# Attention and a mixture of eight experts on one core: when the expert weights are fetched

## The chip, the cores and the metric

The kernel runs on one core of one Trainium2 chip. The metric is the device time of one execution in microseconds (us), less is better. The profile is one execution recorded by the hardware profiler; times in it count from the start of its span.

## The reference

Attention over 4 batches, 8 heads, 768 positions and 64 dimensions a head: three heads attend to everything before them, five only to the first 4 positions and a window of 64. Its output is laid out as 3072 tokens of 512 values, and each token goes through the one expert that its `domain_id` names.

```
scores = where(mask, q @ k.T / sqrt(64), -1e9)       # per batch and head, 768 x 768
attn   = softmax(scores) @ v
x = attn.transpose(0, 2, 1, 3).reshape(3072, 512)    # token, model dimension
for e in range(8):                                   # w1[e]: 512 x 1024, w2[e]: 1024 x 512
    mask = domain_id == e
    out[mask] = relu(x[mask] @ w1[e]) @ w2[e]
```

## The kernel before

**Attention.** The work is cut into 16 steps `n`: 4 batches by 4 pairs of heads. SyncE (SP) loads q, k and v in fp32, GpSimd (POOL) casts them to fp16, TensorE (PE) transposes q and k and multiplies, ScalarE (ACT) takes the exponential, VectorE (DVE) divides and writes the batch's rows into `xb`. After the last step of a batch `store_x` (line 410) sends `xb` to the DRAM tensor `x_tok` through SP's DMA queue. `hooks(n)` (line 751) is called ahead of step `n` and issues the loads and casts of later steps. Its table `ws` (line 764) names the steps at which a weight transfer is issued. At step 14 it issues the first four token gathers, which need only the first three batches.

**Experts.** While attention runs, VectorE works out which token goes to which slot: each expert has 448 slots, two experts make a pair, a pair is seven groups of 128 slots. `load_xe(pr, g)` (line 627) gathers the rows of one group from `x_tok` by an indirect DMA; `x_transpose` (line 640) turns a group so that `layer1(e, c0, c1)` (line 662) can multiply it by `w1` and ScalarE apply the relu; `layer2(e)` (line 697) and `layer2_half(pr)` (line 711) multiply by `w2`, and `finish_group` (line 682) copies 128 result rows to an `oute` tile on VectorE and scatters them to the output by an indirect DMA. The `oute` tiles have 4 buffers, the PSUM tiles of layer 2 have 2.

**Weights.** `load_w(e, 1)` and `load_w(e, 2)` (line 178) fetch `w1[e]` and `w2[e]`. Each reads 2048 KB of fp32 and lands 1024 KB of fp16, so each is a DMA that casts, and GpSimd issues it. There are four buffers for `w1` and four for `w2`; the fifth transfer of a kind waits until the first expert's matmuls have been done.

**What sets the order.** The schedule is written by hand: every engine executes its instructions in the order in which the code emits them. So gathers, weight transfers and scatters all stand in one line on GpSimd, and their packets in one DMA queue (q0 in the profile). The DMAs of this queue use eight completion semaphores in turn (DMASW0 to DMASW7 below): each DMA's issue waits until the DMA eight places ahead of it has landed, and everything behind it on GpSimd waits too.

**The code around the change.** After attention, lines 798 to 830: `store_x(3)`; the gathers of the last three groups (2, 6, 5) of pair 0; `layer1` of experts 0 and 1 on the first 256 slots; the seven gathers of pair 1; five weight transfers; the transposes of groups 2, 6, 5; `layer1` of experts 0 and 1 on their last 192 slots, each followed by a transfer of `w1` for expert 4 or 5; and then the loop over the experts. In iteration `e` of that loop `layer1(e + 2)` stands ahead of `layer2(e)`, even iterations begin with the seven transposes of the next pair and the seven gathers of the pair after it. Two lines show the loop's transfers of weights:

```
            if nxt + 4 < E: load_w(nxt + 4, 1)     # line 826, behind layer1(nxt)
        if e + 4 < E: load_w(e + 4, 2)             # line 829, behind layer2(e)
```

## Time and profile before

| | us |
|---|---|
| median of 3 runs (lowest, highest) | 257.03 (255.66, 266.19) |
| the profiled execution | 254.73 |
| its span | 253.0 |
| busy in the span: PE, VectorE, GpSimd, ScalarE | 202.8, 105.5, 110.2, 92.6 |

The profile's page gives busy time by engine, the span in 40 slices with the clock that the throttle granted to TensorE, the DMA queues and the costliest groups of instructions. Behind the page stand views of the trace: who waited for whom; the instructions of an engine in order of time; the instructions of one line with the time from issue to landing of its DMAs; and busy time, granted clock and DMA share in chosen stretches. In the order of time, brackets at a row's end give the engine's idle time before that row and what ended it. Attention ends near 104 us of the span, the experts' part fills the rest.

### The profile page before, as it was taken

Reading aid. Unit: us, or ns where it says so; the run is one execution under the profiler, and the core shown is the slowest. Engines: PE = TensorE matmul, PEld = TensorE weight load, DVE = VectorE, ACT = ScalarE, POOL = GpSimd, SP = SyncE. Lnnn points to the kernel's source line nnn. Section 1 sums busy time; section 2 is a strip of 40 time slices with the busy share of each in tenths; the row PEclk is TensorE's granted clock in tenths of the full one; section 3 lists DMA queues with packets and bytes.
Section 4 is the critical chain, followed back from the end, with each engine's and each line's share of the span. In section 5 each row is a group of like instructions: output and inputs, shape, how many; then the busy total and the mean of one; then the engine's idle time right before and its main releaser. Section 6 shows DMA issues by size and latency. Waiting matters only on the chain. (4 is left out here: it accounts for less than half of the span.)

```text
span 253.0 us, 4605 instructions
## 1 busy us (share of the span) xinstructions
PE 202.8 (80%) x1871; PEld 120.8 (48%) x1871; DVE 105.5 (42%) x242; ACT 92.6 (37%) x109; POOL 110.2 (44%) x143
## 2 busy tenths in 40 slices
PE   1589899988999999869604999507899979999960
PEld 0246556655666666869401545203545445454420
DVE  1259999997578576501400031004222150403330
ACT  2277547744875876253200504100222305050000
POOL 0557564562455523067932122364757140414550
PEclk9999959997999999997955899956999999999995
DMA  6999999999999842233599999899995856212421
GB/s 218 299 311 305 285 294 254 329 322 244 293 325 226 153 142 72 78 109 97 109 214 216 211 216 216 209 227 237 271 265 174 167 155 135 92 36 84 156 86 37
DMA packets 45467, 49.77 MB, mean 197 GB/s; under 512 B 27263, under 2 KB 38784, under 8 KB 45442
## 3 DMA queue, kind: packets, MB, share of 16 engines
q0 software_dynamic: 7936, 26.75, 45.9%
q1 hardware_dynamic: 36928, 22.02, 31.6%
q10 hardware_dynamic: 578, 0.66, 0.9%
q8 instruction: 16, 0.26, 0.4%
q14 instruction: 9, 0.07, 0.1%
HBM read 56.76 MB, written 10.49 MB: 266 GB/s over the span
## 5 line engine op out<-in xcount | busy, mean ns | idle before, releaser
L332 ACT ACTIVATE eT<-sp 128x1024 f16<-128x1024 f32 (+2 forms) x68 | 60.5, 916 | 35.4 <-PE sp L311 34.8
L678 ACT ACTIVATE hT<-h 128x896 f16<-128x896 f32 (+2 forms) x40 | 30.7, 768 | 96.1 <-PE h L671 96.1
L671 PE MATMUL h<-xT,w 128*128 128x448 f16 (+2 forms) x320 | 54.0, 331 | 11.6 <-DMA w<-in_moe_w_dram 10.8
L684 DVE COPY oute<-o 128x512 f32<-128x512 f32 x24 | 16.6, 692 | 88.5 <-PE o L702 70.1
L702 PE MATMUL o<-w,hT 128*128 128x512 f16 x192 | 44.4, 389 | 10.0 <-DVE oute L684 10.0
L631 POOL DMA_INDIRECT xe<-x_tok,map_i x28 | 28.4, 1013 | 47.9 <-DMA w<-in_moe_w_dram 23.8
L671 PEld LDWEIGHTS <-w 128*128 128x128 f16 x320 | 35.2, 117 | 29.3 <-DMA w<-in_moe_w_dram 11.0
L686 POOL DMA_INDIRECT out_dram<-oute,out_i x28 | 27.9, 997 | 42.4 <-DVE oute L684 37.1
L702 PEld LDWEIGHTS <-hT 128*128 128x128 f16 x192 | 19.0, 99 | 33.6 <-issue 12.4
L386 PE MATMUL av<-ve,eT 128*128 128x65 f16 (+3 forms) x532 | 31.8, 198 | 3.2 <-DVE xb L399 3.2
L386 PEld LDWEIGHTS <-eT 128*128 128x128 f16 (+3 forms) x572 | 25.9, 101 | 13.8 <-issue 4.1
L311 PE MATMUL sp<-qT,kT 64*128 64x192 f16 (+6 forms) x244 | 26.7, 282 | 1.8 <-DVE kT L281 1.2
L311 PE MATMUL sp<-c16s 128*128 128x128 f16 (+1 forms) x132 | 25.9, 279 | 0.4 <-ACT eT L332 0.3
L155 POOL CAST q<-q 128x768 f16<-128x768 f32 x15 | 12.9, 862 | 30.6 <-PE tpq L276 14.5
L281 DVE COPY qT<-tpq 128x768 f16<-128x768 f16 x16 | 15.3, 954 | 7.6 <-PE tpq L276 7.5
L399 DVE TENSOR_TENSOR xb<-av,rcp 128x384 f16<-128x384 f32 x32 | 17.8, 557 | 1.1
L155 POOL CAST k<-k 128x768 f16<-128x768 f32 x16 | 13.5, 842 | 9.9 <-DMA k<-in_k_dram 8.0
L311 PEld LDWEIGHTS <-kT 64*128 64x128 f16 x244 | 9.7, 95 | 16.1 <-issue 7.0
L281 DVE COPY kT<-tpk 128x768 f16<-128x768 f16 x16 | 15.2, 948 | 3.6 <-PE tpk L276 3.6
L176 POOL CAST ve<-v 128x384 f16<-128x384 f32 x32 | 16.0, 528 | 0.7 <-DMA v<-in_v_dram 0.7
L654 DVE COPY xT<-xtp 128x512 f16<-128x512 f16 x24 | 9.1, 418 | 15.2 <-PE xtp L647 14.2
L647 PE MATMUL xtp<-c16s,xe 128*128 128x128 f16 x112 | 10.3, 226 | 6.2 <-DVE xT L654 3.1
(71 smaller groups left out, 123.6 us busy)
## 6 DMA issues: line engine op xcount, KB each, us to landing
w<-in_moe_w_dram POOLq DMA_DIRECT2D x16, 1024.0 KB, 11.3
q<-in_q_dram SPq DMA_DIRECT2D x16, 384.0 KB, 6.0
k<-in_k_dram SPq DMA_DIRECT2D x16, 384.0 KB, 6.0
v<-in_v_dram SPq DMA_DIRECT2D x32, 192.0 KB, 5.7
x_tok<-xb SPq DMA_DIRECT2D x4, 768.0 KB, 6.0
xe<-x_tok,map_i POOLq DMA_INDIRECT x28, 4.8
out_dram<-oute,out_i POOLq DMA_INDIRECT x28, 2.8
c16s<-c ACTq DMA_DIRECT2D x1, 336.5 KB, 4.6
```

What stands on the lines that cost most here:

```text
L155: eng.tensor_copy(out=t[:].rearrange("p t h d -> p h t d"), in_=q32_t[nm, n][:])
L281: nc.vector.tensor_copy(out=d[:], in_=cell["ps"][:].rearrange("d t p -> d p t"))
L311: nc.tensor.matmul(out=sp[:, c : c + w], lhsT=lhsT, rhs=rhs, start=bank not in begun, stop=True, skip_group_check=True,)
L332: nc.scalar.activation(out=eT[n][:, r, c0:c1], in_=sp[:, c0:c1], func=AF.Exp, scale=scale)
L386: nc.tensor.matmul(out=ps[m0:m1, it, :], lhsT=eT[n][kk, r, c : c + w], rhs=rhs, start=(x == 0), stop=(x == len(mms) - 1), skip_group_check ...
L399: nc.vector.tensor_tensor(out=xb[b][:, :, h * D : (h + 1) * D], in0=ps[:, :, 0:D], in1=rcp[:].unsqueeze(2).to_broadcast([P, NSO, D]), op=A ...
L631: nc.gpsimd.indirect_dma_start(out=xe_t[pr][:, g, :], out_offset=None, in_=x_d[0 : 1 + nb * S, :], in_offset=bass.IndirectOffsetOnAxis(ap= ...
L671: nc.tensor.matmul(out=pv[:, a, c0:c1], lhsT=w_t[e, 1][:, c // 2, c % 2, fc * 512 + fr : (fc + 1) * 512 : 4], rhs=xT_t[e][:, c, c0:c1], st ...
L678: nc.scalar.activation(out=hT_t[e][:, 2 * f2 : 2 * f2 + 2, c0:c1], in_=pv[:, :, c0:c1], func=AF.Relu)
L684: nc.vector.tensor_copy(out=o[:], in_=ps[:])
L686: inst = nc.gpsimd.indirect_dma_start(out=out, out_offset=bass.IndirectOffsetOnAxis(ap=out_i[:, s : s + 1], axis=0), in_=o[:], in_offset=None,
L702: nc.tensor.matmul(out=ps[:], lhsT=hT_t[e][:, f, g * P : (g + 1) * P], rhs=w_t[e, 2][:, f // 4, f % 4, :], start=(f == 0), stop=(f == 7),)
```

## The change

Seven weight transfers are issued at other places, and one instruction is added.

- `w2` of expert 0 is issued at step 11 instead of 12, `w1` of expert 2 at step 12, `w2` of expert 1 at step 14, behind the first four gathers.
- After `store_x(3)` and the three gathers of pair 0, `w1` of expert 3 is issued ahead of the gathers of pair 1, and `w2` of expert 2 between its fourth and its fifth gather.
- `w2` of expert 3 is issued between the transfers of `w1` for experts 4 and 5.
- In iteration 6 of the loop over the experts (the last pair begins there) GpSimd executes a `drain`.

```
-        ws = {4: (0, 1), 8: (1, 1), 12: (0, 2)}
+        ws = {4: (0, 1), 8: (1, 1), 11: (0, 2), 12: (2, 1)}
         if n in ws:
             load_w(*ws[n])
         if n == 14:
             for g in (0, 1, 3, 4):
                 load_xe(0, g, 3)
+            load_w(1, 2)
...
         load_xe(0, g)
     for e in range(N_EARLY):
         layer1(e, 0, EARLY)
-    for g in range(NG):
+    load_w(3, 1)
+    for g in range(4):
         load_xe(1, g)
-    load_w(1, 2)
-    for e in (2, 3):
-        load_w(e, 1)
-        load_w(e, 2)
+    load_w(2, 2)
+    for g in range(4, NG):
+        load_xe(1, g)
     for g in (2, 6, 5):
         x_transpose(0, g)
     for e in range(N_EARLY):
         layer1(e, EARLY, CAP)
         load_w(e + 4, 1)
+        if e == 0:
+            load_w(3, 2)
     for e in range(E):
         pr, i = divmod(e, 2)
         nxt = e + 2
+        if e == E - 2:
+            nc.gpsimd.drain()
```

**First place: GpSimd, steps 11 and 12 of attention.** In the rows, `w2_0` is the tile of `w2` of expert 0 (the last number only counts tiles), `q_15` the cast q of step 15, `ve_3` the cast v of batch 3, and the brackets name the semaphores waited for. Before:

```order
L176 CAST ve_3_1493<-v32_3_1_1257 128x6x64 [waits DMAHW4_49]
L176 CAST ve_3_1493<-v32_3_1_1257 128x6x64 [waits DMAHW5_49]
L187 DMA w2_0_1592<-in_moe_w2_dram 128x2x2048
L155 CAST q_15_1693<-q32_15_1482 128x2x6x64 [waits DMAHW3_49,PE_49,Pool_49]
```

Now:

```order
L176 CAST ve_3_1493<-v32_3_0_1138 128x6x64 [waits DMAHW1_49]
L187 DMA w2_0_1499<-in_moe_w2_dram 128x2x2048
L155 CAST q_14_1588<-q32_14_1375 128x2x6x64 [waits DMAHW7_49,PE_49,Pool_49]
L155 CAST k_14_1590<-k32_14_1377 128x2x6x64 [waits DMAHW0_49,PE_49,Pool_49]
L176 CAST ve_3_1493<-v32_3_1_1257 128x6x64 [waits DMAHW4_49]
L176 CAST ve_3_1493<-v32_3_1_1257 128x6x64 [waits DMAHW5_49]
L181 DMA w1_2_1594<-in_moe_w1_dram 128x2x2048
```

`w2_0` has moved one step ahead, and `w1_2` stands where it stood.

**Second place: GpSimd, from the end of the first four gathers.** `xe_0` and `xe_1` are the gathered rows of pairs 0 and 1. Before:

```order
L631 DMA xe_0_1810<-x_tok,map_i_102 128x512 [waits DMAHW0_49]
L631 DMA xe_0_1810<-x_tok,map_i_102 128x512 [waits DMASW0_49]
L631 DMA xe_0_1810<-x_tok,map_i_102 128x512 [waits DMASW1_49]
L631 DMA xe_1_2145<-x_tok,map_i_102 128x512 [waits DMASW2_49,DVE_49,PE_49]
L631 DMA xe_1_2145<-x_tok,map_i_102 128x512 [waits DMASW3_49]
L631 DMA xe_1_2145<-x_tok,map_i_102 128x512 [waits DMASW4_49]
L631 DMA xe_1_2145<-x_tok,map_i_102 128x512 [waits DMASW5_49]
L631 DMA xe_1_2145<-x_tok,map_i_102 128x512 [waits DMASW6_49]
L631 DMA xe_1_2145<-x_tok,map_i_102 128x512 [waits DMASW7_49]
L631 DMA xe_1_2145<-x_tok,map_i_102 128x512 [waits DMASW0_49]
L187 DMA w2_1_2167<-in_moe_w2_dram 128x2x2048 [waits DMASW1_49]
```

Now:

```order
L187 DMA w2_1_1825<-in_moe_w2_dram 128x2x2048 [waits DMASW0_49]
L631 DMA xe_0_1812<-x_tok,map_i_102 128x512 [waits DMAHW0_49,DMASW1_49]
L631 DMA xe_0_1812<-x_tok,map_i_102 128x512 [waits DMASW2_49]
L631 DMA xe_0_1812<-x_tok,map_i_102 128x512 [waits DMASW3_49]
L181 DMA w1_3_2149<-in_moe_w1_dram 128x2x2048 [waits DMASW4_49]
L631 DMA xe_1_2151<-x_tok,map_i_102 128x512 [waits DMASW5_49,DVE_49,PE_49]
L631 DMA xe_1_2151<-x_tok,map_i_102 128x512 [waits DMASW6_49]
L631 DMA xe_1_2151<-x_tok,map_i_102 128x512 [waits DMASW7_49]
L631 DMA xe_1_2151<-x_tok,map_i_102 128x512 [waits DMASW0_49]
L187 DMA w2_2_2164<-in_moe_w2_dram 128x2x2048 [waits DMASW1_49]
```

Three weight transfers (`w2_1`, `w1_3`, `w2_2`) now stand among the gathers instead of behind them.

**Third place: GpSimd, up to the gathers of pair 2** (`xe_2`), directly behind the rows of the second place. Before:

```order
L181 DMA w1_2_2169<-in_moe_w1_dram 128x2x2048 [waits DMASW2_49]
L187 DMA w2_2_2171<-in_moe_w2_dram 128x2x2048 [waits DMASW3_49]
L181 DMA w1_3_2173<-in_moe_w1_dram 128x2x2048 [waits DMASW4_49]
L187 DMA w2_3_2175<-in_moe_w2_dram 128x2x2048 [waits DMASW5_49]
L181 DMA w1_4_2236<-in_moe_w1_dram 128x2x2048 [waits DMASW6_49,PE_49]
L181 DMA w1_5_2278<-in_moe_w1_dram 128x2x2048 [waits DMASW7_49,PE_49]
L631 DMA xe_2_2325<-x_tok,map_i_102 128x512 [waits DMASW0_49]
L631 DMA xe_2_2325<-x_tok,map_i_102 128x512 [waits DMASW1_49]
```

Now:

```order
L631 DMA xe_1_2151<-x_tok,map_i_102 128x512 [waits DMASW2_49]
L631 DMA xe_1_2151<-x_tok,map_i_102 128x512 [waits DMASW3_49]
L631 DMA xe_1_2151<-x_tok,map_i_102 128x512 [waits DMASW4_49]
L181 DMA w1_4_2234<-in_moe_w1_dram 128x2x2048 [waits DMASW5_49,PE_49]
L187 DMA w2_3_2236<-in_moe_w2_dram 128x2x2048 [waits DMASW6_49]
L181 DMA w1_5_2278<-in_moe_w1_dram 128x2x2048 [waits DMASW7_49,PE_49]
L631 DMA xe_2_2325<-x_tok,map_i_102 128x512 [waits DMASW0_49]
L631 DMA xe_2_2325<-x_tok,map_i_102 128x512 [waits DMASW1_49]
```

Seven transfers stood in one block ahead of the gathers of pair 2; three stand there now. From the gathers of pair 2 on, GpSimd's order is the same as before but for the drain, which has no wait of its own and stands behind the scatter of pair 2's last group and ahead of the scatter of pair 3's first.

## Rows read from the trace of the kernel before

**Rows 1.** Page: the span.

```profile
span 253.0 us, 4605 instructions
```

**Rows 2.** Who waited for whom, whole span: us in total, times, longest.

```profile
DVE oute L684 <- DMA out_dram<-oute,out_i: 18.5, 2, 18.2
```

**Rows 3.** PE in order of time from 100 us: start, us, line, what.

```profile
100.54 0.62 PE L647 MATMUL xtp<-c16s,xe 128*128 128x128 f16 x8
...
112.16 0.40 PE L647 MATMUL xtp<-c16s,xe 128*128 128x128 f16 x4 [0.71 <-DMA xe<-x_tok,map_i]
...
125.18 0.40 PE L647 MATMUL xtp<-c16s,xe 128*128 128x128 f16 x4 [1.07 <-DMA xe<-x_tok,map_i]
...
136.36 8.62 PE L671 MATMUL h<-xT,w 128*128 128x448 f16 x32 [10.78 <-DMA w<-in_moe_w_dram]
...
158.02 3.62 PE L702 MATMUL o<-w,hT 128*128 128x512 f16 x16
171.67 3.57 PE L702 MATMUL o<-w,hT 128*128 128x512 f16 x8 [10.04 <-DVE oute L684]
175.04 0.77 PE L647 MATMUL xtp<-c16s,xe 128*128 128x128 f16 x8
...
178.93 6.24 PE L671 MATMUL h<-xT,w 128*128 128x448 f16 x32 [0.39 <-DVE xT L657]
```

**Rows 4.** L187 and L181 in short windows: weight issues, and their time to landing.

```profile
L187 POOL DMA_DIRECT2D w<-in_moe_w_dram x1: 778/778/778, 121.8 to 121.8; - x1
...
DMA to landing us min/median/max: 10.2/10.2/10.2
...
L181 POOL DMA_DIRECT2D w<-in_moe_w_dram x2: 820/830/839, 125.4 to 126.0; - x2
...
DMA to landing us min/median/max: 26.3/30.5/34.7
...
L187 POOL DMA_DIRECT2D w<-in_moe_w_dram x1: 792/792/792, 205.5 to 205.5; - x1
...
DMA to landing us min/median/max: 7.9/7.9/7.9
```

**Rows 5.** POOL in order of time: gathers (L631), weights (L181), scatters (L686).

```profile
92.70 1.09 POOL L631 DMA_INDIRECT xe<-x_tok,map_i  x1 [7.00 <-DVE xb L399]
...
96.76 1.00 POOL L631 DMA_INDIRECT xe<-x_tok,map_i  x1 [0.30 <-issue]
...
111.69 1.00 POOL L631 DMA_INDIRECT xe<-x_tok,map_i  x1 [0.30 <-issue]
...
132.26 1.04 POOL L631 DMA_INDIRECT xe<-x_tok,map_i  x1 [3.99 <-DMA w<-in_moe_w_dram]
...
161.31 0.75 POOL L181 DMA_DIRECT2D w<-in_moe_w_dram  x1 [4.16 <-DMA w<-in_moe_w_dram]
...
234.59 0.98 POOL L686 DMA_INDIRECT out_dram<-oute,out_i  x1 [0.74 <-DVE oute L684]
...
245.18 0.98 POOL L686 DMA_INDIRECT out_dram<-oute,out_i  x1 [0.75 <-DVEq L833]
```

**Rows 6.** Windows: stretch, us, busy PE PEld DVE ACT POOL, clock, DMA share, GB/s.

```profile
92.00:93.00 1.00, 1.00 (x13) 0.45 (x13) 0.65 (x2) 0.20 (x2) 0.30 (x1) 1.00 0.00 0
...
127.00:128.00 1.00, 0.00 (x0) 0.00 (x0) 0.00 (x0) 0.00 (x0) 0.81 (x1) 0.79 1.04 205
...
210.00:220.00 10.00, 10.00 (x57) 4.99 (x57) 2.07 (x3) 2.75 (x3) 2.36 (x3) 1.00 0.42 106
```

**Rows 7.** L411 in two windows: the stores of x_tok, issue and time to landing.

```profile
L411 SPq DMA_DIRECT2D x_tok<-xb x1: 1514/1514/1514, 67.4 to 67.4; - x1
...
DMA to landing us min/median/max: 6.7/6.7/6.7
...
L411 SPq DMA_DIRECT2D x_tok<-xb x1: 384/384/384, 105.1 to 105.1; - x1
...
DMA to landing us min/median/max: 3.7/3.7/3.7
```

More of the change, by code (lines that the diff above doesn't have):

```diff
@@ L763, in hooks @@
             store_x(n // 4 - 1)
-        ws = {4: (0, 1), 8: (1, 1), 12: (0, 2)}
+        ws = {4: (0, 1), 8: (1, 1), 11: (0, 2), 12: (2, 1)}
         if n in ws:
@@ L769, in hooks @@
                 load_xe(0, g, 3)
+            load_w(1, 2)
     for _, fn in t_items(0):
@@ L802 @@
         layer1(e, 0, EARLY)
-    for g in range(NG):
+    load_w(3, 1)
+    for g in range(4):
         load_xe(1, g)
-    load_w(1, 2)
-    for e in (2, 3):
-        load_w(e, 1)
-        load_w(e, 2)
+    load_w(2, 2)
+    for g in range(4, NG):
+        load_xe(1, g)
     for g in (2, 6, 5):
@@ L813 @@
         load_w(e + 4, 1)
+        if e == 0:
+            load_w(3, 2)
     for e in range(E):
@@ L816 @@
         nxt = e + 2
+        if e == E - 2:
+            nc.gpsimd.drain()
         if i == 1:
```

## The prediction

> **What bounds the kernel now.** I read the waits first, then TensorE in order of time, then GpSimd beside it. TensorE is held up twice in the experts' part, for 10.78 and 10.04 us [rows 3]; everything after 175 us runs dense (its engine busy 10.00 of 10.00 us at a clock of 1.00 [rows 6]), and a wait of 0.39 us is what remains there [rows 3].
>
> The first hole ends at 136.36, and its releaser is a weight transfer: `layer1(2)` needs `w1` of expert 2. Seven transfers are issued from 121.8 on, with `w1[2]` second. The first lands at 121.8 + 10.2 = 132.0, the seventh at 126.0 + 34.7 = 160.7 [rows 4], so one lands every (160.7 - 132.0)/6 = 4.8 us, in the order of issue: the DMA queue is the bound here, and TensorE waits for its second item (132.0 + 4.8 = 136.8).
>
> The second hole is the same queue again. A gather of pair 2 waits 3.99 us for a weight, by the eight semaphores used in turn, so GpSimd follows the transfers step by step and issues `w1[6]` only at 161.31 [rows 5], 0.6 after the last of the seven has landed. The first scatters stand behind that. VectorE has four `oute` tiles filled and waits 18.2 us for a scatter to land [rows 2]; TensorE, with both PSUM tiles full, goes on at 171.67 [rows 3]. From the issue of `w1[6]` to there: 171.67 - 161.31 = 10.36 us.
>
> **The change, part by part.** The sum is made against the profiled execution: 253.0 of span [rows 1] and 1.73 around it, 254.73. The three timed runs lie above it, their median by 2.3.
>
> *Steps 11 to 14.* `w2[0]` goes one step forward and costs nothing new: the same issue, the same transfer. `w1[2]` takes its place, and `w2[1]` is issued behind the gather of 96.76, at 97.8 [rows 5]. The queue is empty between (DMA share 0.00 in 92 to 93 [rows 6]), which is the cover: two transfers of 4.8 us go into time in which nothing moved. What they may collide with is the stores of `x_tok`. If the store of batch 2 lands up to 1.6 us later, the first gathers go from 92.7 to 94.3; the last of the four is then issued at 98.4 instead of 96.76, still 2.1 before TensorE begins these transposes at 100.54, and it takes that group last [rows 3, 5]. The store of batch 3 is issued at 105.1 and lands 3.7 later; one that shared the engines with loads took 6.7 [rows 7]. So `w2[1]` (97.8, or 99.4 when the gathers are late, plus 7.9 alone [rows 4]: landed at 105.7 to 107.3) may delay it by 0 to 3.0. I take 0.3, since most of the transfer is over by 105.1. [...]
>
> *Late gathers.* The last gather of pair 0 ends at 111.69 + 1.00 + 0.3 = 113.0 [rows 5]. `w1[3]` is issued there and lands 7.9 later, at 120.9 (a transfer alone [rows 4]). Four gathers of pair 1 follow, 1.3 us each with the 0.30 between them [rows 5], to 119.0; they land behind `w1[3]`, by 122.5, about when TensorE turns to them (now 121.6, four transposes a group). `w2[2]` is issued at 119.0 and lands at 126.9. Groups 4 to 6 are issued by 123.7 but lie behind it in the queue. A gather lands an eighth of a weight's bytes and reads a sixteenth, so 0.3 to 0.6 us of 4.8 each (an estimate from rows 4); with 0.4 the last lands at 128.1. Its transposes (0.40, as at 125.18) and the wait for VectorE's copy behind them (0.39, as at 178.93 [rows 3]) lead to 128.9. So a hole of some 4 us is left ahead of `layer1(2)`, now for gathers, and it starts at 128.9 instead of 136.36: 7.5 earlier. `w1[2]` and the rest of its weights are long there.
>
> *TensorE's path from there.* Before, 136.36 to the end of the sixteen matmuls at 158.02 + 3.62 = 161.64 took 25.28 us, with `layer1(2)` at 8.62 instead of the 6.24 that the same 32 matmuls take at 178.93 [rows 3], because the granted clock had fallen to its lower level (1.2 of 2.4 GHz) during the hole, within 127 to 128, two to three us after the last transposes [rows 3, 6]. A hole of 4 us will probably still let it fall, so I keep 8.62: 128.9 + 25.28 = 154.2. With 6.24 it is 151.8.
>
> *The queue's path.* Behind the gather at 128.1 stand three transfers instead of seven: 132.9, 137.7, 142.5. `w1[6]` is issued 0.6 later, at 143.1, and 10.36 after that TensorE may go on: 153.4. That is earlier than 154.2, so the second hole closes, just. If the clock does not fall, TensorE is there at 151.8 and waits 1.6.
>
> *After the hole.* The eight matmuls of 171.67 ran until 175.04, 3.37 us at the low clock; sixteen at the high one take 3.62, so eight take 1.8 [rows 3]. They end at 154.2 + 1.8 = 156.0 instead of 175.04: 19.0 earlier. From there on TensorE works on what has landed, as before: GpSimd's order is the same and its transfers keep their distance to TensorE.
>
> *The drain.* GpSimd's scatter of 234.59 comes 0.74 after the one before, and so do most of the seven up to 245.18 with 0.75 [rows 5]. So below 0.74 us the drain is free, and up to about 7 x 0.74 = 5.2 the last scatter is not moved by it directly. No row shows a drain. Below, its cost is nothing (it waits for no semaphore). Above I take the 253.0 - 246.2 = 6.8 that the program needs after the last scatter's issue [rows 1, 5], which holds everything that ends a program: less the idle 0.74 at its place, 6.1, if the four `oute` tiles pass it on to TensorE before the later idle times take it back. So 0 to 6; I take 0, as the value nearest to the 0.30 us that GpSimd shows between two of its instructions [rows 5]. The Trainium skill ("VectorE: DVE Perf Modes", section "The DRAIN you can't avoid") gives some 0.012 us for the drains of a program's beginning and end, by which the sum stays as it is; no run so far shows it.
>
> **Sum.** 254.73 - 19.0 = 235.7 for a profiled execution, 257.03 - 19.0 = 238.0 by the median of the runs. I predict 237.
>
> **The rivals.**
> - *The queue's path is longer than I count.* By another count three transfers fewer stand behind 121.8: 171.67 - 3 x 4.8 = 157.3, 3.1 later than TensorE's path, so 16 saved: 240. For it: each transfer is used to the full, and I have put the new chain together from pieces. Against it: the chain also starts at 113.0 instead of 121.8.
> - *The last gathers of pair 1 wait for one transfer more* (`w1[4]`, if the queue doesn't keep order closely): `layer1(2)` at 133.7, and 14 saved: 242. Against it: transfers landed in order, 4.8 apart.
> - *Attention or its stores pay for the early weights.* `w1[2]` and `w2[1]` are new ahead of 105. If each delayed TensorE by its full 4.8, 9.4 of the 19.0 would be left: 247. Against it: the idle queue of 92 to 93 and a queue with nothing in it between the old transfer and the gathers.
> - *The drain decides, and the kernel is slower.* Its place is ahead of the last pair's scatters. To cost more than 19.0 it would have to hold GpSimd some 19.0 + 5.2 = 24 us; then the time is 257 and more. Nothing in GpSimd's rows is near that, its longest single wait for a transfer here is 4.16 [rows 5].
> - *No change to be measured* (within 2%): the second hole opens again in full behind the first, 254.73 - 7.5 and the low clock once more, about 247 to 252.
>
> **How the numbers follow.** My forecast, 17.5 to 21 saved: 0.65. Queue longer: 0.13. Gathers one transfer later: 0.06. Attention pays: 0.08. Within 2%: 0.05. Slower: 0.03. A measurement of this kernel tells some 2% (5 us) from no change, so faster has 0.92. The range takes the forecast with both ways of clock, 21 saved from 254.73, 233.7, and reaches up to the first two rivals by the median, 257.03 - 14 = 243: 233 to 243.
>
> **What would show it.** `layer1(2)` starting near 129 with a short wait for `xe` ahead of it, not for `w`; groups 4 to 6 of pair 1 landing just behind `w2[2]`; `w1[6]` issued near 143; no wait, or one under 2 us, of layer 2 for `oute` near 154; the tail from there 78 us as now; the scatters of the last pair with no idle time over 0.74 more than now. I would be wrong if attention's end moved from 104, if the store of batch 3 landed much after 109, or if GpSimd stood at the drain.

## The result

| | before | after |
|---|---|---|
| median, first set of runs (lowest, highest) | 258.37 (255.66, 266.19) | 242.5 (242.14, 243.21) |
| ratio to before, 95% interval | | 0.946 (0.941 to 0.952) |
| median, second set of runs (experiment r_after) | 257.26 (253.21, 260.54) | 240.66 (238.53, 242.61) |
| ratio to before, 95% interval | | 0.941 (0.923 to 0.960) |
| the profiled execution | 254.73 | 242.54 |
| its span | 253.0 | 240.7 |

The changed kernel is faster. The medians hold all runs and differ by 16 to 17 us; the ratios are taken over the runs near each kernel's fastest alone (for before in the first set 257.03 and 255.66 us) and make the gain 13.8 us in the first set and some 15 us in the second. The forecast was 237 us, 19.0 less than before.

The page of the profile after, the answer to [rows 1]:

```profile
span 240.7 us, 4606 instructions
```

Who waited for whom in the profile after (total us, times, longest), the answer to [rows 2] and the wait of TensorE for VectorE behind it:

```profile
DVE oute L684 <- DMA out_dram<-oute,out_i: 13.3, 3, 9.4
...
PE o L702 <- DVE oute L684: 2.6, 2, 1.3
```

VectorE still waits 9.4 us for a scatter, but TensorE waits for VectorE only 1.3 us at a time. TensorE in order of time, the answer to [rows 3]:

```profile
109.23 8.37 PE L671 MATMUL h<-xT,w 128*128 128x256 f16 x64
...
132.99 1.03 PE L647 MATMUL xtp<-c16s,xe 128*128 128x128 f16 x8 [3.94 <-DMA xe<-x_tok,map_i]
135.27 0.61 PE L647 MATMUL xtp<-c16s,xe 128*128 128x128 f16 x4 [1.25 <-DMA xe<-x_tok,map_i]
136.26 7.55 PE L671 MATMUL h<-xT,w 128*128 128x448 f16 x32 [0.39 <-DVE xT L657]
...
156.86 3.62 PE L702 MATMUL o<-w,hT 128*128 128x512 f16 x16
161.76 1.89 PE L702 MATMUL o<-w,hT 128*128 128x512 f16 x8 [1.29 <-DVE oute L684]
163.49 0.61 PE L647 MATMUL xtp<-c16s,xe 128*128 128x128 f16 x8
```

The holes of 10.78 and 10.04 us [rows 3] have become 3.94 + 1.25 us, now for gathers, and 1.29 us. Yet `layer1(2)` starts at 136.26, the same place as before (136.36), because attention's end (the first matmul of layer 1) moved from 104.21 to 109.23. GpSimd in order of time, the answer to [rows 5], with the casts of the v tiles and the weights of steps 11 and 12 ahead:

```profile
75.90 0.31 POOL L173 MEMSET ve<- 128x48 f16 x1
...
76.93 0.72 POOL L187 DMA_DIRECT2D w<-in_moe_w_dram  x1
...
81.34 0.72 POOL L181 DMA_DIRECT2D w<-in_moe_w_dram  x1
...
92.72 0.52 POOL L176 CAST ve<-v 128x384 f16<-128x384 f32 x1 [6.29 <-DMA v<-in_v_dram]
...
114.61 1.05 POOL L631 DMA_INDIRECT xe<-x_tok,map_i  x1 [13.20 <-SPq L838]
...
118.29 0.78 POOL L181 DMA_DIRECT2D w<-in_moe_w_dram  x1
...
124.35 0.78 POOL L187 DMA_DIRECT2D w<-in_moe_w_dram  x1
...
128.11 1.00 POOL L631 DMA_INDIRECT xe<-x_tok,map_i  x1 [0.30 <-issue]
...
151.16 0.75 POOL L181 DMA_DIRECT2D w<-in_moe_w_dram  x1 [4.15 <-PE o2h L716]
```

Three instructions serve as marks below, besides TensorE's going on after the second hole. The memset of `ve_3` (75.90 here) opens step 11: up to it both kernels execute the same code. Attention's end is the first L671. "The first late gather" is the one behind the store of batch 3 (114.61 here). The same marks in the profile of before:

```profile
74.71 0.31 POOL L173 MEMSET ve<- 128x48 f16 x1
...
104.21 7.25 PE L671 MATMUL h<-xT,w 128*128 128x256 f16 x64
...
109.08 1.00 POOL L631 DMA_INDIRECT xe<-x_tok,map_i  x1 [11.32 <-SPq L833]
```

In the second profiles (r_before, r_after) they stand at 73.97, 103.48, 108.33 and at 80.53, 110.03, 115.42. The last mark is the end of the eight matmuls behind the second hole, that is, the first transposes after it: 175.04 and 163.49, in the second profiles 174.14 and 163.91. The length of each stage, and what the forecast had for its change:

| stage | before, twice | after, twice | difference, twice | forecast |
|---|---|---|---|---|
| start to the memset | 74.71, 73.97 | 75.90, 80.53 | +1.19, +6.56 | 0 |
| memset to attention's end | 29.50, 29.51 | 33.33, 29.50 | +3.83, -0.01 | 0 |
| attention's end to the first late gather | 4.87, 4.85 | 5.38, 5.39 | +0.51, +0.54 | +0.3 |
| first late gather to the end of the eight matmuls | 65.96, 65.81 | 48.88, 48.49 | -17.08, -17.32 | -19.3 |
| from there to the end of the span | 77.96, 77.96 | 77.21, 76.79 | -0.75, -1.17 | 0 |
| span | 253.0, 252.1 | 240.7, 240.7 | -12.3, -11.4 | -19.0 |

The part behind attention repeats within 0.4 us, and it is the change's gain. The first two rows are the puzzle: they take 5 to 6.5 us of it away in the profiles. The runs lose less: rows three to five gain 17.3 and 18.0 us together, some 3 us more than the 13.8 to 15 us that the ratios show. The experiments ask what moves attention's end, what the queue's path is made of, and what the drain costs.

### The profile page after: what moved, and what is told of

Same layout as the page of the kernel before. It is cut to its first block, busy times and chain, and to the rows that moved or that the text cites. A ratio compares the mean times of both kernels' runs of the same rounds, so it can differ in the third digit from the quotient of the medians.

```text
span 240.7 us, 4606 instructions
## 1 busy us (share of the span) xinstructions
PE 203.6 (85%) x1871; PEld 121.6 (51%) x1871; DVE 107.0 (44%) x242; ACT 92.5 (38%) x109; POOL 110.7 (46%) x143
## 4 chain that ended last, share of the span: by engine, by line
issue 21%; DMA 18%; POOL 9%; POOLq 2%; PE 1%; DVE 1%; DVEq 0%
DMA w<-in_moe_w_dram 14%; POOL out_dram L686 6%; DMA xe<-x_tok,map_i 3%; POOL w L187 1%; DMA out_dram<-oute,out_i 1%; POOL w L181 1%; PE o L702 1%; POOL xe L631 1%; POOLq L927 1%; DVE oute L684 1%; POOLq L821 1%; POOLq L686 0%; POOLq L838 0%; POOLq L631 0%; POOLq L187 0%
## 5 line engine op out<-in xcount | busy, mean ns | idle before, releaser
L671 PE MATMUL h<-xT,w 128*128 128x448 f16 (+2 forms) x320 | 53.2, 326 | 1.8 <-DVE xT L657 1.2
L686 POOL DMA_INDIRECT out_dram<-oute,out_i x28 | 27.9, 998 | 42.0 <-DVE oute L684 36.2
L702 PE MATMUL o<-w,hT 128*128 128x512 f16 x192 | 42.9, 379 | 2.6 <-DVE oute L684 2.6
L671 PEld LDWEIGHTS <-w 128*128 128x128 f16 x320 | 34.3, 116 | 19.7 <-issue 3.3
L631 POOL DMA_INDIRECT xe<-x_tok,map_i x28 | 28.5, 1019 | 32.2 <-SPq L838 13.2
L386 PE MATMUL av<-ve,eT 128*128 128x65 f16 (+3 forms) x532 | 33.0, 201 | 4.7 <-DVE xb L399 3.8
L386 PEld LDWEIGHTS <-eT 128*128 128x128 f16 (+3 forms) x572 | 26.9, 103 | 15.7 <-DVE xb L399 4.6
L647 PE MATMUL xtp<-c16s,xe 128*128 128x128 f16 x112 | 11.2, 241 | 10.0 <-DMA xe<-x_tok,map_i 6.9
L311 PEld LDWEIGHTS <-kT 64*128 64x128 f16 x244 | 9.7, 95 | 17.1 <-issue 7.3
```

What stands on the lines that cost most here:

```text
L311: nc.tensor.matmul(out=sp[:, c : c + w], lhsT=lhsT, rhs=rhs, start=bank not in begun, stop=True, skip_group_check=True,)
L386: nc.tensor.matmul(out=ps[m0:m1, it, :], lhsT=eT[n][kk, r, c : c + w], rhs=rhs, start=(x == 0), stop=(x == len(mms) - 1), skip_group_check ...
L631: nc.gpsimd.indirect_dma_start(out=xe_t[pr][:, g, :], out_offset=None, in_=x_d[0 : 1 + nb * S, :], in_offset=bass.IndirectOffsetOnAxis(ap= ...
L671: nc.tensor.matmul(out=pv[:, a, c0:c1], lhsT=w_t[e, 1][:, c // 2, c % 2, fc * 512 + fr : (fc + 1) * 512 : 4], rhs=xT_t[e][:, c, c0:c1], st ...
L686: inst = nc.gpsimd.indirect_dma_start(out=out, out_offset=bass.IndirectOffsetOnAxis(ap=out_i[:, s : s + 1], axis=0), in_=o[:], in_offset=None,
L702: nc.tensor.matmul(out=ps[:], lhsT=hT_t[e][:, f, g * P : (g + 1) * P], rhs=w_t[e, 2][:, f // 4, f % 4, :], start=(f == 0), stop=(f == 7),)
```

## Experiment 1: what moves attention's end

**r_before and r_after**: both kernels once more, without an edit, for second profiles on one chip.

> The kernel before once more, unchanged, for a second profile of it. What is open: in the shown profile of before attention's end (the first matmul of layer 1) came 29.5 us after the memset of the last batch's v tile and TensorE kept its full clock there; the changed kernel took 33.3, and before with nothing but the drain 34.2. Theory 1 (the shown profile of before was a quick one at that place, and the early weights cost little there): this profile takes 33 to 34 us over that stretch, with TensorE's clock at its lower level and a wait of TensorE ahead of layer 1, and its span is 2 to 5 us above 253.0. Theory 2 (the early weights cost the 4 to 5 us): 29 to 30 again, as in the shown profile. Both: 62 to 63 us from the first gather behind the store of batch 3 to the end of the second hole, and 81 to 82 from there to the end of the span.

> The changed kernel once more, unchanged, on the same chip as the others of this set. Theory 1 (the place of attention's end varies by itself): 33 to 34 us from the memset of the last batch's v tile to attention's end, as before shows in its second profile. Theory 2: the same 33, but 29 to 30 in before. Both: 47 us from the first gather behind the store of batch 3 to the end of the second hole, 79 from there to the end, a drain of 6.6 us ahead of the last pair and one of 3.9 at the end. Time 242 to 244.

Before took 257.08 us at the median, after 240.66. Neither theory had it right: before again takes 29.51 us from the memset to attention's end, as theory 2 said, but so does after. GpSimd's and TensorE's rows of r_after in order of time:

```profile
80.53 0.31 POOL L173 MEMSET ve<- 128x48 f16 x1
...
110.03 7.25 PE L671 MATMUL h<-xT,w 128*128 128x256 f16 x64
```

Here the difference lies ahead of the memset, where nothing was changed. The page of the profile shows where it comes from: TensorE's granted clock in 40 slices of the span (9 is full speed, 5 half). First before, then r_after:

```profile
PEclk9999959997999999997955899956999999999995
```

```profile
PEclk9999995599557999999999599999999999999998
```

r_after has the clock at its lower level in four slices of the first 12 (72 us), before in one slice of its first 12 (76 us). In the first profile of after the clock stayed up there, but fell at attention's end. Windows of that profile (stretch, us, busy time of PE, PEld, DVE, ACT, POOL, granted clock, DMA share, GB/s):

```profile
98.00:100.00 2.00, 1.99 (x26) 1.06 (x25) 0.00 (x0) 0.44 (x1) 1.39 (x3) 1.00 0.26 78
...
102.00:104.00 2.00, 1.53 (x13) 0.81 (x11) 0.52 (x1) 1.80 (x3) 0.00 (x0) 0.50 0.98 135
```

**e3_before_drain** (its drain is discussed below; up to attention's end it executes the code of before).

```diff
         nxt = e + 2
+        if e == E - 2:
+            nc.gpsimd.drain()
```

> The kernel before with the drain alone. Theory A (early drain takes work off the end): the drain takes some 6.6 us, the end drain falls from 6.1 to 3.9, TensorE waits about 1.3 us for a scatter, the span is 252 to 253 against 253.0. Theory B (lost time): 254 or more, end drain unchanged.

Its profile has the same fall at attention's end without any early weight. GpSimd and TensorE in order of time, then a window of it:

```profile
80.54 0.31 POOL L173 MEMSET ve<- 128x48 f16 x1
...
114.78 9.35 PE L671 MATMUL h<-xT,w 128*128 128x256 f16 x64
```

```profile
106.00:108.00 2.00, 2.00 (x19) 0.97 (x18) 0.20 (x1) 0.73 (x1) 0.00 (x0) 0.50 0.03 8
```

34.24 us from memset to attention's end, with TensorE busy 2.00 of 2.00 us at half its clock.

**e2_ws_12_13**: the early weights one step later each.

```diff
-        ws = {4: (0, 1), 8: (1, 1), 11: (0, 2), 12: (2, 1)}
+        ws = {4: (0, 1), 8: (1, 1), 12: (0, 2), 13: (2, 1)}
```

> The changed kernel with w2[0] back at step 12 and w1[2] at step 13. Theory A (w2[0] at step 11 is issued within a us of the last v load and slows it, 15.4 us to landing instead of 5.6; GpSimd waits 6.3 for it, and attention ends 5.0 late): the v load lands in 6 to 7 us, the wait at the last cast goes, attention ends at 104 to 106, and the span is 3 to 5 us shorter, 236 to 238. Theory B (two transfers in a row ahead of the store of batch 2 do it, at whatever step): the gathers still wait, attention's end stays at 108 to 110, the span at 240 to 242.

247.17 us at the median (ratio 0.956, 0.949 to 0.963). In the same set the change without its drain (e1 below) has 0.934 (0.926 to 0.943), so this is slower. The wait of the v cast for its load (6.29 us in after) is gone, but the first gathers now wait for the store of batch 2, which SP issued at 91.5: they read the `x_tok` that it writes. (The releaser that the row names differs from profile to profile.) GpSimd in order of time:

```profile
102.00 1.09 POOL L631 DMA_INDIRECT xe<-x_tok,map_i  x1 [11.73 <-DVE vs L749]
```

They start 10.5 us after that store's issue, against 5.1 in before (87.6, 92.70) and 6.8 in after (88.8, 95.58); TensorE waits 0.45 + 0.95 + 0.87 + 0.97 us for them. A later place was worse here; that this wait is the reason isn't shown, since e2 takes 33.52 us from the memset to attention's end and e1 33.86. That the late v load is no harm by itself is seen in the profile of e6 (below, the same attention): GpSimd and TensorE there.

```profile
76.80 0.31 POOL L173 MEMSET ve<- 128x48 f16 x1
...
93.90 0.52 POOL L176 CAST ve<-v 128x384 f16<-128x384 f32 x1 [2.77 <-DMA v<-in_v_dram]
...
106.31 7.25 PE L671 MATMUL h<-xT,w 128*128 128x256 f16 x64
```

The cast comes later than in after (17.1 us behind the memset instead of 16.8), and attention's end is 29.51 us behind the memset.

**t_before and t_after**: both kernels cut off behind attention; all that follows `layer1` of experts 0 and 1 on their first 256 slots is left out.

```diff
     for e in range(N_EARLY):
         layer1(e, 0, EARLY)
...
+    o = opool.tile([P, DM], FP32, tag="oute", name="oute_cut")
+    for e in range(N_EARLY):
+        nc.vector.tensor_copy(
+            out=o[:, e * EARLY : (e + 1) * EARLY], in_=hT_t[e][:, 7, 0:EARLY]
+        )
+    nc.sync.dma_start(out=out[0:P, :], in_=o[:])
```

> The kernel before, cut off behind attention: the late gathers of pair 0 and layer 1 of experts 0 and 1 on their first 256 slots stay, the rest of the experts' part is left out (one tile of layer 1 is written out instead), so its time is that of attention and some 15 us more: 118 to 126 us. It is the base for the next run; its spread shows what attention alone varies by. Both theories: no difference to the first 105 us of the kernel before.

> The changed kernel cut off at the same place, so that only the three early weight transfers differ (w2 of expert 0 at step 11, w1 of expert 2 at 12, w2 of expert 1 behind the first gathers). Theory 1 (the early weights cost attention nothing but the 0.5 us by which the store of the last batch lands later; where attention's end came later, the clock had fallen by chance): the median is within 1.5 us of the cut kernel before, and its profile has 29.5 us from the memset of the last batch's v tile to attention's end wherever the clock stays at its upper level. Theory 2 (they make attention longer, by themselves or by bringing the clock's fall oftener): 2.5 to 4 us above the cut kernel before.

Medians of 123.12 (119.43 to 124.27) and 124.29 us (121.29 to 126.69): 1.17 us apart, inside what theory 1 allows; their fastest runs are 1.86 us apart. Rows of t_before, then of t_after, GpSimd and TensorE, and each one's clock:

```profile
77.00 0.31 POOL L173 MEMSET ve<- 128x48 f16 x1
...
106.50 7.25 PE L671 MATMUL h<-xT,w 128*128 128x256 f16 x64
```

```profile
PEclk9999999999999999999967999999999999999965
```

```profile
80.96 0.31 POOL L173 MEMSET ve<- 128x48 f16 x1
...
110.46 7.25 PE L671 MATMUL h<-xT,w 128*128 128x256 f16 x64
```

```profile
PEclk9999999999995558999855559999999999999996
```

From memset to attention's end 29.50 us in both. The 4 us between the two profiles lie ahead of the memset and go with the fallen clock, in code that is the same.

**What follows.** Where the clock stayed up, attention from step 11 on takes 29.5 us with the early weights (r_after, e5, e6, e7, e8, t_after) and without them (before, r_before, e10, t_before). So the early weights cost attention nothing there; the late gathers start 0.5 us later behind its end. Where it took 32 to 34 us (after, e1, e2 and e4 with early weights, e3 without), the layer behind it ran at a lowered clock, 8.4 to 9.4 us instead of 7.25, so the clock had fallen at attention's end. e9 below lies between: 29.95 us, and 8.88 for that layer. That is the clock's lower level (1.2 of 2.4 GHz), and it is reached in attention in runs of either kernel. The lateness goes with the set of runs rather than with the weights: e1 to e4 ran on one chip, and all four profiles have it, e3 without early weights among them (the chip of the first profiles isn't on record); of the ten profiles taken on two other chips (r_before, r_after, e5 to e10, t_before and t_after) none took more than 29.95 us. The start of the memset varies as much without early weights (73.97 to 80.54 us in five profiles) as with them (74.19 to 80.96 in eleven).

Open is whether the lower clock comes a little oftener with the early weights. The cut kernels differ by 1.17 us at the median and by 1.86 at their fastest, within a spread of 5 us; e10 below, with two of the early weights taken back, is 2 us quicker than its stages say; and the whole runs gain some 3 us less than the stages behind attention's end. All three point the same way, so a cost of 1 to 3 us isn't excluded.

## Experiment 2: what the queue's path is made of

**e4_only_ws**: before, with `w2[0]` and `w1[2]` at steps 11 and 12 and nothing else.

```diff
-        ws = {4: (0, 1), 8: (1, 1), 12: (0, 2)}
+        ws = {4: (0, 1), 8: (1, 1), 11: (0, 2), 12: (2, 1)}
...
     load_w(1, 2)
-    for e in (2, 3):
-        load_w(e, 1)
-        load_w(e, 2)
+    load_w(2, 2)
+    load_w(3, 1)
+    load_w(3, 2)
```

> The kernel before with w2[0] at step 11 and w1[2] at step 12, all else in its old place (w2[1], w2[2], w1[3], w2[3] in a block behind the gathers of pair 1, no drain). Theory A (w2[0] at step 11 delays the last v load): GpSimd waits some 6 us for v, attention ends at 108 to 109 instead of 104.2; the queue's block is one transfer shorter, so TensorE leaves its second hole at 171.7 - 4.8 + 4.5 = 171.4, span 252 to 253, nothing gained. Theory B (the delay came from the later transfers): attention ends at 104 to 105, second hole left at 167, span 247 to 249.

252.49 us (ratio 0.977, 0.971 to 0.984). From the first late gather (111.71) to the second hole's end (169.17) 57.5 us instead of 62.6: one transfer less in the line is worth 5.1 us. The first hole, ahead of `layer1(2)`, is closed and the second has grown to 11.70: closing the first alone doesn't help beyond that transfer. (TensorE sits idle for 2.97 and 2.02 us some 10 us ahead of that, in the layers on the last 192 slots, with no wait that the profile shows; why is open.)

**e10_only_late**: the changed kernel, with the early part undone.

```diff
-        ws = {4: (0, 1), 8: (1, 1), 11: (0, 2), 12: (2, 1)}
+        ws = {4: (0, 1), 8: (1, 1), 12: (0, 2)}
...
-            load_w(1, 2)
...
-    load_w(3, 1)
+    load_w(2, 1)
     for g in range(4):
         load_xe(1, g)
-    load_w(2, 2)
+    load_w(1, 2)
     for g in range(4, NG):
         load_xe(1, g)
+    load_w(3, 1)
+    load_w(2, 2)
```

> The changed kernel with the early part undone: w2 of expert 0 at step 12 as before, and w1 of expert 2 and w2 of expert 1 behind attention, where w1 of expert 3 and w2 of expert 2 stood; these two follow behind the gathers of pair 1. Theory A (each transfer that is taken out of the line behind attention is worth its 4.8 to 5 us, and ahead of attention's end the two cost nothing): layer 1 of expert 2 starts as in the changed kernel, 21 to 22 us after the first late gather, the second hole is 10 us longer (11 to 12 us), from the first late gather to its end 57 us instead of 47, the time is 10 us above the changed kernel's, 251 to 252. Rival B (the early transfers cost attention what they save behind it, in part): attention's end comes 3 us or more earlier than in the changed kernel, and the time is under 249.

TensorE in order of time behind the second hole:

```profile
168.63 3.57 PE L702 MATMUL o<-w,hT 128*128 128x512 f16 x8 [10.47 <-DVE oute L684]
```

From the first late gather (111.62) 57.0 us, and `layer1(2)` starts 22.0 after it, both as theory A said: two transfers more, 10 us more. The median, 248.79 us (ratio 0.958, 0.950 to 0.967), is 6 to 8 us above the two medians of the change instead of 9 to 10, and by this and by an attention's end at 106.76 rival B's numbers are met as well. But the earlier end lies ahead of the memset (77.26 against 80.53 in r_after); from there it is 29.50 us in both. So theory A holds for what was changed, and 2 us of the runs' difference are not accounted for; the cut kernels above were made for that.

**e5_w2_behind**: `w2[2]` behind all seven gathers of pair 1.

```diff
-    for g in range(4):
-        load_xe(1, g)
-    load_w(2, 2)
-    for g in range(4, NG):
+    for g in range(NG):
         load_xe(1, g)
+    load_w(2, 2)
```

> The changed kernel with w2 of expert 2 issued behind all seven gathers of pair 1 instead of between the fourth and the fifth. Theory A (behind attention the DMA queue is the bound, and the gathers' place among the transfers only decides where TensorE waits): the wait ahead of layer 1 of expert 2 shrinks from 3.9 + 1.3 us to under 1, that layer starts 4 us earlier after the first late gather, the second hole grows from 1.3 to 5 to 6 us, and from the first late gather to the second hole's end it stays 47 us; the time stays within 1 us of the changed kernel's. Rival B (TensorE's path through the late gathers sets the time, the queue has room): the second hole stays under 2 us and the time falls by 3 to 4 us, to 238 or 239.

TensorE in order of time:

```profile
131.74 7.90 PE L671 MATMUL h<-xT,w 128*128 128x448 f16 x32 [0.39 <-DVE xT L657]
...
163.08 3.25 PE L702 MATMUL o<-w,hT 128*128 128x512 f16 x8 [6.78 <-DVE oute L684]
```

`layer1(2)` starts 17.1 us after the first late gather (114.60) instead of 21.6, and the second hole is 6.78 instead of 1.29 us: 48.5 us to its end, no gain. The time is 243.68 us (ratio 0.948, 0.920 to 0.976). Theory A holds in its mechanism: the queue is the bound in the changed kernel, and rival B falls. The hole is longer than the 5 to 6 us it gave, and the stage 1.3 to 1.7 us longer than the change's instead of equal.

The time from issue to landing in r_after (short windows of L187 and L181) shows what the queue's path is made of; the rows are `w2[2]`, issued at 125.13, `w1[4]` at 129.88, `w2[3]` at 130.62, `w1[5]` at 131.34:

```profile
DMA to landing us min/median/max: 8.5/8.5/8.5
...
DMA to landing us min/median/max: 11.0/11.0/11.0
...
DMA to landing us min/median/max: 15.5/15.5/15.5
...
DMA to landing us min/median/max: 19.6/19.6/19.6
```

They land at 133.6, 140.9, 146.1 and 150.9. The last gather of pair 1, between the first two, has landed by 135.98, where TensorE takes it. `w1[6]` is issued at 151.52, 0.6 after the last of them. (Its row in after names TensorE as the releaser; in e5, where TensorE is 4 us further on by then, the same wait of 4.15 us is put down to the weight.)

## Experiment 3: the drain

Rows of the drain's line and of the program's end in after (engine, times; ns shortest/median/longest; first and last start), then GpSimd in order of time behind it, the answer to the scatters of [rows 5]:

```profile
L821 POOLq DRAIN  x1: 6603/6603/6603, 221.0 to 221.0; - x1
...
L927 POOLq DRAIN  x3: 46/109/3885, 235.7 to 240.4; - x3
```

```profile
228.51 0.98 POOL L686 DMA_INDIRECT out_dram<-oute,out_i  x1 [6.25 <-DVE oute L684]
...
236.26 0.99 POOL L686 DMA_INDIRECT out_dram<-oute,out_i  x1 [0.30 <-issue]
```

The drain takes 6.6 us. Scatters pile up behind it, TensorE waits 1.27 us for an `oute` tile once (at 232.13), the scatters then follow at 0.30 us of idle time instead of 0.74, and the last one is late. The program's end has a GpSimd drain of its own in every kernel; in before it is 6.09 us long, here 3.89. The row of before, which was there to be read ahead of the change:

```profile
L922 POOLq DRAIN  x3: 46/109/6090, 246.0 to 252.7; - x3
```

**e1_no_drain**: the change without the drain.

```diff
-        if e == E - 2:
-            nc.gpsimd.drain()
```

> The changed kernel without the drain. In the changed kernel the drain takes 6.6 us on GpSimd, and the drain at the program's end takes 3.9 instead of 6.1. Theory A (a drain clears work that grows with the DMAs issued since the last one, so an early drain takes it off the end): without it the end drain is 6.1 again, the 1.3 us wait of TensorE ahead of its last eight matmuls goes, and the span is 0.5 to 1 us longer, 241.2 to 241.7. Theory B (the early drain is lost time): the span is 1.3 us or more shorter, below 239.5, and the end drain stays at 3.9.

The end's drain is 6.09 us again. From the end of the second hole to the last scatter's end it takes 72.8 us instead of 75.5, and from there to the end of the span 6.8 instead of 3.4: with the drain the sum is 78.9, without it 79.65. The drain loses 2.7 us and saves 3.4. The time is 244.47 us at the median (ratio 0.934, 0.926 to 0.944); a difference of 0.7 us isn't seen in it. **e3_before_drain** (above) has a drain of 6.6 us ahead of the last pair and one of 3.7 at the end; its time, 260.94 us, ratio 0.994 (0.984 to 1.004), shows no difference either. From the end of the eight matmuls to the end of the span it takes 79.0 us, with one layer at a lower clock (7.93 instead of 6.24): 77.3 without that, an estimate, against 77.96 in before, so 0.7 gained again.

**e6_drain_it4**: the drain two iterations earlier.

```diff
-        if e == E - 2:
+        if e == E - 4:
             nc.gpsimd.drain()
```

> The changed kernel with the drain in iteration 4 of the loop over the experts instead of 6, where GpSimd had 9.9 us of idle time ahead of a scatter. Theory A (a GpSimd drain has a length of its own, which grows with the DMAs that GpSimd issued since the last one; what one takes ahead of the end is saved at the end): the drain takes 6 to 6.6 us and nothing waits for it, the last pair's scatters stand 1.7 us apart again, TensorE's wait of 1.27 us behind the last half layer is gone, the end's drain takes 4 to 4.5 instead of 3.9; from the end of the second hole to the last scatter's end 72.8 us instead of 75.5, and the time falls by 2 to 2.6 us, to 240. Rival B (the end's drain is short because the drain stood just ahead of the last pair): the end's drain is near 6 us again and the time stays within 0.7 us.

239.03 us (237.74 to 239.67), ratio 0.936 (0.920 to 0.952), 1.6 below the change in the same set at the median; the interval of its ratio (0.923 to 0.960) overlaps this one, so the runs alone don't tell the two apart. In the profiles the drain's new place shows: from the end of the eight matmuls to the end of the span it takes 74.6 us here, 77.2 and 76.8 in after and r_after. Rows of the drain's line and of the end:

```profile
L821 POOLq DRAIN  x1: 11060/11060/11060, 192.9 to 192.9; - x1
```

```profile
L927 POOLq DRAIN  x3: 46/109/2855, 234.1 to 237.5; - x3
```

Nothing waits for the drain, TensorE's wait of 1.27 us is gone, and the last scatter ends 72.8 us after the second hole. So the place is right. The lengths are not as expected: 11.06 us in the loop and 2.86 at the end. The transfer of `w2[7]`, issued at 193.6 just ahead of the drain, took 7.9 us to land (201.5); the drain ended at 204.0.

**e8_drain_first**: the drain as the program's first instruction on GpSimd.

```diff
+    nc.gpsimd.drain()
     load_qk(0)
...
-        if e == E - 2:
-            nc.gpsimd.drain()
```

> The changed kernel with its GpSimd drain at the program's beginning, ahead of every DMA of GpSimd, instead of ahead of the last pair. What is open: the end's drain took 6.1 us without another drain, 3.5 to 3.9 with one in iteration 6 and 2.9 with one in iteration 4. Theory C (the first GpSimd drain of a program pays once, whatever went before): the one at the beginning takes some 2 to 3 us in which GpSimd has nothing to do, the end's drain takes 2.9, and the time is that of the kernel with the drain in iteration 4, 239 to 240. Rival D (a drain has to work off the DMAs that GpSimd issued since the last one): the first is short, under 1 us, the end's is 6.1, and the time is that of the changed kernel without a drain, 241 to 242.

```profile
L727 POOLq DRAIN  x1: 41/41/41, 0.7 to 0.7; - x1
```

```profile
L926 POOLq DRAIN  x3: 46/109/6095, 233.2 to 239.9; - x3
```

41 ns, and the end's drain is 6.10 us, as without any. Theory C falls. The lengths themselves mix two parts. In every profile the drain outlasts the last packet of GpSimd's queue (q0, from the traces' packet records), so a part of it is waiting: 8 us in e6, for `w2[7]`. What it goes on for behind that packet grows with the number of DMAs that GpSimd issued since the last drain: 0.7 to 0.8 us behind 7 (the end in after and r_after), 0.9 to 1.0 behind 10 to 14 (t_before, t_after, the end in e6), 2.7 behind 58 (e6 in the loop), 4.0 behind 65 (iteration 6), 4.1 to 4.3 behind 72 (the end in before, r_before, e1 and e8). The end's drain in after is longer than in e6, 3.9 against 2.9, because it starts at 235.67, ahead of the last scatter (236.26). What the second part is made of is open.

## A version that beats both

**e9_late_w1_only**: `w1` of experts 6 and 7 behind the scatters of layer 2, so that these needn't lie behind it in the queue, and the drain in iteration 4.

```diff
-            if nxt + 4 < E:
-                load_w(nxt + 4, 1)
         layer2(e)
+        if nxt + 4 < E:
+            load_w(nxt + 4, 1)
```

> The changed kernel with two of these moves: the transfers of w1 for experts 6 and 7 behind the scatters of layer 2, and the drain in iteration 4; w2 of expert 2 stays between the gathers. Theory A (queue and TensorE's path are within 1 to 2 us of each other here): the second hole closes, but TensorE's own path through the late gathers (first late gather to the second group of layer 2 at 46 us) becomes the bound, so only 0.4 to 1.3 us are won against the kernel with the drain in iteration 4 alone: 238. Rival B (no gain or a loss): 239 or more.

238.31 us (ratio 0.924, 0.915 to 0.933); the second hole is closed (the 24 matmuls of layer 2 run in one piece), and the eight matmuls are done 48.7 us after the first late gather. That is no earlier than in after (48.5 and 48.9), and the eight begin near 47 us (48.7 less the 1.7 that they take) where 46 was expected: with the hole closed, TensorE's own path through the late gathers is the bound, as theory A said, and in this profile `layer1(2)` ran at a lower clock, 8.75 us instead of the 7.5 of after, which took back what the hole gave. The interval overlaps that of the kernel with the drain in iteration 4 alone (e6), so a gain over it isn't shown.

**e7_late_w1**: the same, and `w2[2]` behind the gathers as in e5.

> The changed kernel with three moves: w2 of expert 2 behind all seven gathers of pair 1, the transfers of w1 for experts 6 and 7 behind the scatters of layer 2 instead of ahead of them, the drain in iteration 4. Theory A (the queue is the bound up to the second hole: the first scatters lie behind five transfers and w1 of expert 6): with that transfer out of their way the scatters are issued when w1 of expert 5 has landed and land 2 to 3 us later, so the second hole is under 1 us though layer 1 of expert 2 starts 4 us earlier; from the first late gather to the second hole's end 42 us instead of 47 to 48.5, and the time 234 to 236. Rival B (the queue has room there, or the late w1 opens a hole in iteration 4): 238 or more, with a wait of TensorE for weights of experts 4 to 7 near 195 us.

TensorE in order of time:

```profile
131.38 7.92 PE L671 MATMUL h<-xT,w 128*128 128x448 f16 x32 [0.39 <-DVE xT L657]
...
156.26 1.89 PE L702 MATMUL o<-w,hT 128*128 128x512 f16 x8 [0.29 <-DVE oute L684]
...
162.25 7.93 PE L671 MATMUL h<-xT,w 128*128 128x448 f16 x32 [0.39 <-DVE xT L657]
```

237.71 us (235.05 to 238.79), ratio 0.9165 (0.907 to 0.927): the lowest ratio of all. The mechanism is as theory A said: 41.9 us from the first late gather (114.35) to the second hole's end, both holes gone, no wait for weights later. In this profile 3.4 us of it go again where two layers ran at a lower clock, 7.93 instead of 6.24 us each (the one at 162.25, and that of expert 6), and its time is 238.79 us. The median misses the expected 234 to 236; that the lower clock is the reason in the other runs too isn't shown. e7 and e9 can't be told apart by their intervals.

## Why the prediction was off, step by step

The direction was right, and behind attention the mechanism too; the gain was 13.8 to 15 us by the ratios, 16 to 17 by the medians, instead of 19.0. 242.5 us (240.66 in the second set) stands for the forecast 237, at the upper end of the range, and 0.946 of the 257.03 that the forecast started from is 243.2, just above it. Two terms of the sum failed: the queue's path, which was 2.4 to 2.9 us too short, and attention, whose change was put at nothing.

- **The first hole** was forecast to end with `layer1(2)` 19.5 us after the first late gather (128.9 against 109.08 + 0.3). It took 21.65 (136.26 - 114.61). `w2[2]` landed 8.5 us after its issue instead of 7.9 and the three gathers behind it took 2.3 us (133.6 to 135.9) where I had 1.2. It waits for `xe` and not for `w`, as said.
- **TensorE's path** from there was forecast with `layer1(2)` at 8.62 and took 7.55; the lower clock came, but not for the whole layer. That gives 1.07 back.
- **The queue's path** is the term that failed behind attention: `w1[6]` was forecast to be issued 33.7 us after the first late gather (143.1 - 109.4); it was 36.55 (151.16 - 114.61), 36.1 in r_after. Behind `w2[2]` the next three transfers landed at 140.9, 146.1, 150.9: the first of them 5.0 after the gathers, then 5.2 and 4.8, for 4.8 each. With the 0.6 of `w2[2]`, its issue 0.1 later and the 1.1 of the gathers that is the 2.4 us missing in r_after. From the issue of `w1[6]` to TensorE's going on 10.6 us, forecast 10.36. The forecast had the queue done 0.8 us ahead of TensorE (153.4 against 154.2), which swallowed a part. So the rival "queue longer" was the right one in its mechanism, at a smaller price (2.0 to 2.2 us in the stage's end instead of 3.1), and the second hole was left at 1.29 us.
- **Attention and its stores.** The cover that I named held where the clock stays up: there attention takes 29.50 us from the memset on with and without the early weights. The late gathers came 0.5 us later behind attention's end, forecast 0.3, but not by the forecast's way: the store of batch 3 landed 3.7 us after its issue in before, r_before, after and r_after alike, and the 0.5 lies between its landing and the first gather. Why isn't shown. The 6.7 us of the other store of [rows 7] were no measure of what a weight does to a store: while that one ran, 67.4 to 74.1, GpSimd's queue moved nothing, and it shared SP's own queue with the loads of q, k and v. The rival "attention pays" is what the profile of after looked like, with attention's end 5.0 us late; the runs show the same lateness without early weights (e3), and none behind the memset with them (r_after). In part the rival is still open, see the last point.
- **The drain** was put at 0, with a cost of 0 to 6 us as its bounds. It is 6.6 us long and makes the last scatter 2.7 us late; that it nets out at 0.7 us gained was luck: the 3.4 us saved at the end's drain had not been thought of, though the trace of before held that drain with its 6.09 us.
- **Attention's length and the base.** The sum was made against 254.73, a profile in which attention went quickly, and put no change on attention. With the stage behind attention as measured (17.1 less instead of 19.3), the late gathers at +0.5 and the tail at -0.75 the change is worth 17.3 us; from 256.3 us, the mean of the two runs of before in the first ratio, this gives 239.0, and the mean of after was 242.6. In the second set it is 18.0 against some 15. So some 3 us are missing ahead of the first late gather. The two profiles of after show 5.0 and 6.5 us there, in stretches at the lower clock: 3.83 behind the memset in one, 6.56 ahead of it, in code that is the same, in the other. Whether the early weights have a part in it or the clock alone stays open; the experiments leave room for 1 to 3 us.

## What to carry to other kernels

Where one queue carries everything, count it from one event on, transfer by transfer with its own landing times, and let the small DMAs behind a large one count too; moving a transfer out of that line was worth its 5 us each time (e4, e10), and moving it within the line was worth nothing (e5) until the first scatters no longer lay behind `w1[6]` (e7 against e9, in the profiles). Before a late mark is blamed on a change, look for it in a second profile of the unchanged code: a stage whose clock varies needs a mark ahead of the change and one behind it. The drain that the end of this program executes anyway could be paid for earlier, where GpSimd was idle (e6): read the end of the trace too before an instruction is priced.

## What the runs showed of the hardware

- A GpSimd drain took 41 ns ahead of all DMAs, 6.60 us in iteration 6, and 11.06 us behind a weight transfer that landed 7.9 us after its issue; the end's drain fell from 6.09 to 2.86 us when there was one in iteration 4. Behind the queue's last packet it went on for 0.7 us after 7 DMAs and for 4.2 us after 72.
- The last load of v was late in some profiles with two weight transfers under way: the cast waited 6.29 us for it in after, and not at all in r_after with the same code; in e6 the cast came as late as in after and TensorE was not late for it.
- TensorE's granted clock fell from 1.00 to 0.50 of its full speed in attention in profiles of either kernel, at different places, with the engine busy 1.99 of 2.00 us just before (98 to 100 in after).
